# High and low parts of the projected rows in a DRAM region each, 128 rows outermost

## The chip, the cores and the metric

The kernel runs on one core of one Trainium2 chip. The metric is the device time of one execution in microseconds, lower is better. A run of 831.89 us in this document is the median of three executions (829.76 to 833.49).

## What is computed

The reference gates two blocks over the same input `x` (2048 rows of 512): sliding-window attention with 32 heads of 16 columns, and a gated linear unit.

```python
def _A_ref(x, wqkv, wo):
    H = 32; Dh = D // H; W = 256
    q, k, v = ...                       # x @ wqkv, split into heads
    scores = jnp.einsum("bhqd,bhkd->bhqk", q, k) * (Dh ** -0.5)
    mask = (idx[:, None] - idx[None, :] >= 0) & (idx[:, None] - idx[None, :] < W)
    p = _softmax(jnp.where(mask[None, None], scores, -1e9), axis=-1)
    return merge_heads(jnp.einsum("bhqk,bhkd->bhqd", p, v)) @ wo

def _B_ref(x, w_gate, w_up, w_down):
    return (_sigmoid(x @ w_gate) * (x @ w_up)) @ w_down      # F = 1376

g = _sigmoid((x * gate_w).sum(-1, keepdims=True))
return g * _A_ref(...) + (1 - g) * _B_ref(...)
```

## The kernel before

All products are made from split operands: each float32 value is a high part (rounded by ScalarE) and a low part (the rest, by VectorE), and a product is the sum of three matmuls of such parts.

**The work.** Heads come in 8 groups of 4 (`NG`, `HG`), tokens in 16 blocks of 128 (`NB`) and in 4 chunks of 512 (`NC`). A *step* `s` is one group and one chunk, 32 in all. For each step the q and k rows are projected into a PSUM tile `pj`; `proj_hi` (L270) and `proj_lo` (L280) leave the high and low parts in SBUF tiles `sh` and `sl` of 128 partitions by 1024 columns, which hold two neighbouring steps, a *pair*.

**The ring.** The score matmuls read a tile `ring` with 3 slots (`RING`), each for one pair. In a slot, every fourth partition holds a row-wise different thing: rows 1 to 3 of each four hold high and low parts of q and k, row 0 holds the running maximum of a query (with its high and low part), so that one matmul of 64 rows gives the score and subtracts the maximum as well. The parts have to change partitions on the way from `sh` and `sl` to the ring. For the first two pairs DMAs do this directly from SBUF (`stack_build`). From the third pair on (14 pairs) the way leads through DRAM: once both halves of a pair are made, `proj_lo` queues two stores of 512 KB to `stack_scratch`, one for `sh` and one for `sl` (L287), and `stack_load` (L289) queues five loads from it into the ring, 1.5 MB in all, with a small fill from `fill_scratch`.

**The loop.** The main loop (L795) runs over *units* `u`, one per group and block, 128 of them and 10 more. In a unit, `s_part` makes scores of a block of queries against up to three blocks of keys, for their maximum alone (matmul L342, then VectorE's reduction L348). `st_part` makes, 9 units later, the scores again, keys as rows, with the maximum subtracted by the ring's rows (matmul L390, then ScalarE's exponential L395 into `pbuf`). Between these, half-height matmuls of the projections and of the gated linear unit (`gu`, L255) fill TensorE.

**The way of the maxima.** Every four units there is a *visit* (L813): `pv_part` multiplies the probabilities with v (L424), `max_split` makes the negated maxima on VectorE and transposes them into `nt` (L363), and `max_store` (L366) sends `nt` to DRAM. `max_load` (L373) then brings them back into row 0 of the ring in two DMAs. The next block of `st_part` needs them.

**The queue.** Nearly all DMAs are issued by SyncE (SP) in the order written here, by `run_dmas` (L316) over the list `later` and over the loads in `sdma`. SP waits, before each, until its data are ready, and all that is written behind it waits too. In a visit the order is: what is left in `later`, `max_store`, then the output of the attention (`ob` to `oT_scratch` in four DMAs, its sums to `sum_scratch`), then `max_load`, then up to three loads of the stack. The stores of a pair stand in `later` some units ahead of every second visit.

After the 128 units comes a last stage (L965): the gated hidden rows are read back from `gu_scratch` and `tail_scratch`, multiplied with `w_down`, and the attention's output with `wo`.

Of the kernel before, what the change touches and what calls it, by code (L numbers as in the profile page):

```python
# [7 lines left out]
F32 = mybir.dt.float32  # L8
# [6 lines left out]
P = 128  # L15
# [21 lines left out]
RING = 3  # L37
CH2 = 2 * CH
# [3 lines left out]
QB = 32  # L42
# [15 lines left out]
def gated_mix_kernel(  # L58
# [11 lines left out]
    nc = tc.nc  # L70
# [22 lines left out]
    gu_d = nc.dram_tensor("gu_scratch", (2, NFM, P, T), F32, kind="Internal").ap()  # L93
    tail_d = nc.dram_tensor("tail_scratch", (NB, P, 2 * TF), F32, kind="Internal").ap()
    max_d = nc.dram_tensor("max_scratch", (NG * NC, P // QB, HG, 2, 4, QB), F32, kind="Internal").ap()
    stack_d = nc.dram_tensor("stack_scratch", (RING, 4, 2, QB, CH2), F32, kind="Internal").ap()
    fill_d = nc.dram_tensor("fill_scratch", (2, CH2), F32, kind="Internal").ap()

    cpool = ctx.enter_context(tc.tile_pool(name="cpool", bufs=1))
# [37 lines left out]
    with ExitStack() as actx:  # L137
# [44 lines left out]
        def fill_rows(r, which, v):  # L182
            dst = ring[r].bitcast(F32).rearrange("(a r) j f -> r a j f", r=32)[0, :, 2 * which:2 * which + 2]
            return dst, fill_d[v:v + 1].partition_broadcast(8).rearrange("(a j) o f -> a j (o f)", j=2)
# [65 lines left out]
        later = []  # L250
# [29 lines left out]
        def proj_lo(s):  # L280
            sh, sl = parts.pop(s)
            nc.vector.tensor_tensor(sl, pj.pop(s), sh.bitcast(F32), op=ALU.subtract)
            t = s // 2
            made[t] = made.get(t, 0) + 1
            if t > 1 and made[t] == 2:
                for low, v in enumerate(stg.pop(t)):
                    later.append((stack_d[t % RING, :, low], v.bitcast(F32)))  # L287

        def stack_load(t):  # L289
            assert made[t] == 2  # L290
            rows = ring[t % RING].bitcast(F32).rearrange("(a r) j f -> r a j f", r=4)
            dmas = [fill_rows(t % RING, 0, 0)]
            if t < RING:
                dmas.append(fill_rows(t, 1, 1))
            for r, low, js in ((0, 0, (0, 4)), (1, 1, (0, 2)), (1, 0, (2, 4)), (2, 0, (0, 2)), (2, 1, (2, 4))):
                js = slice(*js)
                dmas.append((rows[r + 1, :, js], stack_d[t % RING, js, low].rearrange("j a f -> a j f")))
            return dmas

        def stack_build(t):  # L300
# [141 lines left out]
        def proj(s):  # L442
            for k in range(3 * ND):
                proj_mm(s, k)
            proj_hi(s)
            proj_lo(s)
# [28 lines left out]
        for s in (0, NC):  # L475
            for k in range(3 * ND):
                proj_mm(s, k)
        proj_hi(0)
        proj_lo(0)
        proj_raw(NC)  # L480
        proj(1)
# [87 lines left out]
        def proj_post(s):  # L569
            proj_hi(s)  # L570
            behind.append(lambda: proj_lo(s))
# [223 lines left out]
        for u in range(N):  # L795
# [11 lines left out]
            if u % 8 == 1 and u > 8 and u // 8 + 1 < NP:  # L807
                sdma = stack_load(u // 8 + 1)
# [112 lines left out]
        def blocks(v):  # L921
            return v.rearrange("p (d t) -> p d t", d=ND)

        def free_slot(h, d, c):
            return slot(h, d, c).bitcast(F32)
# [6 lines left out]
        rows = [blocks(free_slot(0, k, 3)) for k in range(2)]  # L932
# [32 lines left out]
        for n, (c, f) in enumerate(steps):  # L965
# [45 lines left out]
            for t in range(4):  # L1011
                r = slice(t * QB, (t + 1) * QB)
# [67 lines left out]
```

## Time and profile before

| what | value |
|---|---|
| median of 3 runs | 831.89 us (829.76 to 833.49) |
| the profiled execution's own time | 831.66 us |
| its span, first to last instruction | 829.9 us |
| TensorE (PE) busy | 757.0 us, 91% of the span |
| VectorE (DVE) busy | 488.0 us, 59% |
| ScalarE (ACT) busy | 425.0 us, 51% |
| GpSimd (POOL) busy | 167.0 us, 20% |
| DMA moved | 118.30 MB, mean 143 GB/s |
| stores to `stack_scratch` | 28 of 512 KB |
| loads from `stack_scratch` into the ring | 14 of 512 KB, 56 of 256 KB |
| mean granted TensorE clock | 0.942 |

The chain that ended last is the work followed back from the last instruction, at each step to what released it. "Idle before" is the time an engine did nothing ahead of an instruction. `PEclk` is the share of TensorE's full clock that was granted. `DMA share` is the mean busy share of the core's 16 DMA engines: 0.25 is four engines' worth. SPq is the time that SP took to issue a DMA.

### The profile page before, as it was taken

What the parts mean: (1) busy time and instruction counts of PE and PEld (TensorE: products, weight loads), DVE (VectorE), ACT (ScalarE), POOL (GpSimd) and SP (SyncE); (2) the same over time, 40 slices, a digit from 0 to 9 for tenths busy, and PEclk for the clock granted to TensorE, in tenths of its full rate; (3) what the DMA queues carried; (4) which work ended last, traced back from release to release, by engine and by line L of the source; (5) the groups of instructions that cost most, each with busy time, mean ns of one, the idle gap of its engine ahead of it and who ended that gap; (6) DMA issues with size and microseconds to landing.
All of it is one profiled execution on the core that took longest, in us unless ns stands there. A gap on an engine that the chain in (4) does not pass through costs nothing.

```text
span 829.9 us, 17381 instructions
## 1 busy us (share of the span) xinstructions
PE 757.0 (91%) x6298; PEld 625.1 (75%) x6298; DVE 488.0 (59%) x1455; ACT 425.0 (51%) x890; POOL 167.0 (20%) x255
## 2 busy tenths in 40 slices
PE   9997889798988879897989879949999999999998
PEld 7785777676867768776877758738787888888886
DVE  5386547364756557364646556635685577858482
ACT  6323555364646447454645555626566655535341
POOL 6001222132213123221323222212233200000000
PEclk9999899898989899898989898979999999999999
DMA  8332343434343444535344334443355798869451
GB/s 282 87 110 77 96 141 125 153 111 138 116 140 85 150 114 137 164 99 170 94 138 126 114 99 157 149 127 111 123 163 169 231 232 227 241 146 269 118 126 51
DMA packets 99166, 118.30 MB, mean 143 GB/s; under 512 B 46190, under 2 KB 58990, under 8 KB 99080
## 3 DMA queue, kind: packets, MB, share of 16 engines
q1 hardware_dynamic: 98936, 117.06, 47.9%
q8 instruction: 49, 0.80, 0.4%
q14 instruction: 37, 0.30, 0.1%
q10 hardware_dynamic: 144, 0.13, 0.0%
HBM read 67.34 MB, written 46.67 MB: 137 GB/s over the span
## 4 chain that ended last, share of the span: by engine, by line
PE 74%; DMA 21%; DVE 3%; issue 1%; ACT 0%; SPq 0%; DVEq 0%; ACTq 0%
PE gu L255 20%; DMA max_scratch<-nt 14%; PE pj L255 8%; PE pv L424 6%; PE s L342 5%; PE st L390 5%; PE tp L559 5%; PE pd L88 4%; PE pd L86 4%; PE pd L87 4%; DMA ring<-max_scratch 4%; PE vh L596 2%; DVE junk L348 2%; PE pa L86 2%; PE pa L87 2%; PE pa L88 2%
## 5 line engine op out<-in xcount | busy, mean ns | idle before, releaser
L348 DVE CUSTOM_DVE_ANT_0 junk<-s,mask 128x384 f32<-128x384 f32 (+2 forms) x512 | 272.2, 532 | 239.0 <-PE s L342 181.2
L395 ACT ACTIVATE pbuf<-st 128x384 f32<-128x384 f32 (+2 forms) x512 | 241.6, 477 | 261.9 <-PE st L390 183.3
L255 PE MATMUL gu<-xh,w 64*128 64x512 f32 x1152 | 299.0, 407 | 0.0
L390 PE MATMUL st<-ring 64*128 64x384 f32 (+2 forms) x536 | 177.5, 347 | 65.4 <-DMA ring<-max_scratch 65.4
L255 PE MATMUL gu<-xl,w 64*128 64x512 f32 x576 | 196.1, 406 | 0.0
L401 POOL TENSOR_SCALAR_AFFINE_SELECT pbuf<-pbuf 128x512 f32<-128x512 f32 x128 | 85.0, 664 | 470.5 <-ACT pbuf L395 429.5
L255 PEld LDWEIGHTS gu<-xh,w 64*128 64x128 f32 x1152 | 169.5, 194 | 9.8
L342 PE MATMUL s<-ring 64*128 64x384 f32 (+2 forms) x536 | 170.2, 336 | 0.5 <-DVE mx L348 0.3
L390 PEld LDWEIGHTS st<-ring 64*128 64x128 f32 x536 | 102.4, 196 | 75.7 <-issue 70.5
L342 PEld LDWEIGHTS s<-ring 64*128 64x128 f32 x536 | 100.2, 194 | 19.4 <-DVE mx L348 5.4
L255 PEld LDWEIGHTS gu<-xl,w 64*128 64x128 f32 x576 | 97.2, 195 | 3.5
L255 PE MATMUL pj<-xh,wqh 64*128 64x512 f32 (+1 forms) x228 | 95.2, 444 | 0.0
L255 PE MATMUL pj<-xl,wqh 64*128 64x512 f32 (+1 forms) x228 | 93.5, 436 | 0.0
L424 PE MATMUL pv<-pbuf,V 128*32 128x384 f32 (+2 forms) x1408 | 84.5, 386 | 0.5 <-POOL pbuf L401 0.5
L255 PE MATMUL pj<-xh,wql 64*128 64x512 f32 (+1 forms) x228 | 80.7, 442 | 0.0
L424 PEld LDWEIGHTS pv<-pbuf,V 128*32 128x32 f32 x1408 | 41.4, 110 | 42.0 <-issue 30.7
L407 POOL TENSOR_SCALAR_AFFINE_SELECT pbuf<-pbuf 128x512 f32<-128x512 f32 x112 | 72.8, 650 | 0.0
L86 PE MATMUL pd<-ring,hb 128*128 128x512 f32 x160 | 62.3, 389 | 0.0
L88 PE MATMUL pd<-ring,hb 128*128 128x512 f32 x160 | 62.3, 389 | 0.0
L87 PE MATMUL pd<-ring,hb 128*128 128x512 f32 x160 | 62.2, 389 | 0.0
L82 ACT CAST hb<-V 128x512 fp32r<-128x512 f32 x40 | 24.9, 622 | 57.3 <-DVE V L760 45.5
L255 PEld LDWEIGHTS pj<-xh,wql 64*128 64x128 f32 (+1 forms) x228 | 48.8, 218 | 2.3
(127 smaller groups left out, 1122.2 us busy)
## 6 DMA issues: line engine op xcount, KB each, us to landing
gu_scratch<-sp SPq DMA_DIRECT2D x72, 256.0 KB
V<-gu_scratch SPq DMA_DIRECT2D x36, 512.0 KB
ring<-stack_scratch SPq DMA_DIRECT2D x56, 256.0 KB
stack_scratch<-sh SPq DMA_DIRECT2D x14, 512.0 KB
stack_scratch<-sl SPq DMA_DIRECT2D x14, 512.0 KB
ring<-stack_scratch SPq DMA_DIRECT2D x14, 512.0 KB
guraw<-in_wgu_dram SPq DMA_DIRECT2D x18, 256.0 KB
oT_scratch<-ob SPq DMA_DIRECT2D x128, 32.0 KB
```

What stands on the lines that cost most here:

```text
L86: mm(ps, lh, rh, start=first, stop=False)
L87: mm(ps, lh, rl, start=False, stop=False)
L88: mm(ps, ll, rh, start=False, stop=last)
L255: return mm(pt, (wl if w == 2 else wh)[r, d], (xl if w == 1 else xh)[r, d, c * CH:(c + 1) * CH], start=k == 0 and not second, stop=k == 3 ...
L342: mm(pt[:, (k - k0) * P:(e - k0) * P], lhsT, blk(g, k, hh, 1, e - k), start=k == k0, stop=e == i + 1, skip_group_check=True,)
L348: nc.vector.tensor_tensor_reduce(junk[:, 0:n], pt[:, 0:n], mask[:, 3 * P - n:], scale=1.0, scalar=NEG, op0=ALU.add, op1=ALU.max, accum_out ...
L390: mm(pt[:, (q - j) * P:(e - j) * P], lhsT, blk(g, q, hh, 0, e - q), start=q == j, stop=e == last, skip_group_check=True,)
L395: exps.append(nc.scalar.activation(p_blk(u, hh, 0, n), pt[:, 0:n * P].rearrange("p (b t) -> p b t", t=P), AF.Exp, scale=SCALE,))
L401: nc.gpsimd.affine_select(pbuf[:, s0], pbuf[:, s0], pattern=[[0, HG], [1, P]], compare_op=ALU.is_ge, fill=0.0, base=0, channel_multiplier=-1,)
L407: nc.gpsimd.affine_select(old, old, pattern=[[0, HG], [-1, P]], compare_op=ALU.is_gt, fill=0.0, base=0, channel_multiplier=1,)
L424: mm(pv[32 * hh:32 * hh + 32, (q - q0) * P:(e - q0) * P], Vf[:, v:v + 32], p_blk(g * NB + j, hh, q - j, e - q), start=j == j0, stop=j == q ...
L559: return mm(tp[b][:, 0:TW], (xl if w == 1 else xh)[r, d, b * P:(b + 1) * P], tw[d][int(w == 2)][r, 0:TW], start=k == 0 and not second, sto ...
```

## The change

The scratch tensor gets another shape. Before, it had for each ring slot 4 groups of 32 rows, and within each group first the high and then the low part. Now each slot has two regions, all 128 rows of the high parts and then all 128 rows of the low parts. The store of `sh` or `sl` was written with the shape 4 by 32 by 1024 on the DRAM side (its groups were 256 KB apart); now it is 128 rows of 1024 on both sides, in one piece of 512 KB. The loads read the same rows in the same shape, from their new places.

```diff
-    stack_d = nc.dram_tensor("stack_scratch", (RING, 4, 2, QB, CH2), F32, kind="Internal").ap()
+    stack_d = nc.dram_tensor("stack_scratch", (RING, 2, P, CH2), F32, kind="Internal").ap()
@@ proj_lo
                 for low, v in enumerate(stg.pop(t)):
-                    later.append((stack_d[t % RING, :, low], v.bitcast(F32)))
+                    later.append((stack_d[t % RING, low], v.bitcast(F32)))
@@ stack_load
                 js = slice(*js)
-                dmas.append((rows[r + 1, :, js], stack_d[t % RING, js, low].rearrange("j a f -> a j f")))
+                dmas.append((rows[r + 1, :, js], stack_d[t % RING, low].rearrange("(j a) f -> a j f", a=QB)[:, js]))
```

The instructions of PE, DVE, ACT and POOL stay what they were and where they were. On SP the 28 stores change their shape and nothing changes its place. This is the first visit with such stores, on SP; the names are tiles, `nt` the transposed maxima, `sh` and `sl` the high and low parts:

```order
 L366 DMA max_scratch<-nt_804 128x32
-L316 DMA stack_scratch<-sh_448 4x32x1024
-L316 DMA stack_scratch<-sl_449 4x32x1024
+L316 DMA stack_scratch<-sh_448 128x1024
+L316 DMA stack_scratch<-sl_449 128x1024
 L316 DMA ring<-fill_scratch 4x2x1024 x2
 L316 DMA ring<-stack_scratch 32x4x1024
```

Nothing moved: the stores' outermost dimension goes from 4 to 128, and the load behind them keeps its shape. The next pair's stores, on SP too, stand behind a `max_load` and ahead of stores of `gu` (`sp`):

```order
 L316 DMA sum_scratch<-ob_1124 4x512
 L373 DMA ring<-max_scratch 4x16x32 x2
-L316 DMA stack_scratch<-sh_1140 4x32x1024
-L316 DMA stack_scratch<-sl_1141 4x32x1024
+L316 DMA stack_scratch<-sh_1140 128x1024
+L316 DMA stack_scratch<-sl_1141 128x1024
 L316 DMA gu_scratch<-sp_1_0_1255 128x512
```

Here too only the shape of the two stores differs, and the DMAs around them are in the order they had.

## The prediction

> **What bounds the kernel now.** I read what TensorE waited for, then the chain of waits around one such wait, then SyncE's queue through two neighbouring visits, and then the DMA share in short windows.
>
> ```profile
> PE st L390 <- DMA ring<-max_scratch: 65.4, 14, 10.4
> ```
>
> TensorE (PE) stood idle for 65.4 us in 14 waits, the longest 10.4, all at the score matmul L390 and all for the load of the maxima into the ring. There are also 14 pairs whose parts go through `stack_scratch`. The chain around one wait (start, duration, what):
>
> ```profile
> 258.41 12.49 DMA max_scratch<-nt
> ```
>
> The store of 16 KB of maxima takes 12.49 us to land. What stands before the store is in SyncE's queue, for a visit without stores of a pair (245.00) and the next one with them (258.41):
>
> ```profile
> 245.00 0.32 SPq L366 DMA_DIRECT2D max_scratch<-nt  x1
> 246.43 1.71 SPq L316 DMA_DIRECT2D oT_scratch<-ob  x4
> 248.18 0.57 SPq L316 DMA_DIRECT2D sum_scratch<-ob  x1
> 248.87 1.17 SPq L373 DMA_DIRECT2D ring<-max_scratch  x2
> ...
> 254.25 0.55 SPq L316 DMA_DIRECT2D stack_scratch<-sh  x1
> 255.45 0.54 SPq L316 DMA_DIRECT2D stack_scratch<-sl  x1
> 258.41 0.33 SPq L366 DMA_DIRECT2D max_scratch<-nt  x1
> 261.81 3.77 SPq L316 DMA_DIRECT2D oT_scratch<-ob  x4
> 265.62 0.51 SPq L316 DMA_DIRECT2D sum_scratch<-ob  x1
> 270.98 1.20 SPq L373 DMA_DIRECT2D ring<-max_scratch  x2
> ```
>
> In the plain visit the load is issued 3.87 us after the store of the maxima, so that store had landed by then. In the visit behind a pair's stores it is 12.57 us, and even the issue of four small DMAs takes 3.77 us instead of 1.71. The DMA share tells why:
>
> ```profile
> 252.50:253.30 0.80, 0.80 (x12) 0.71 (x10) 0.53 (x3) 0.80 (x3) 0.80 (x2) 1.00 0.85 328
> 261.60:262.60 1.00, 1.00 (x12) 0.91 (x10) 0.62 (x3) 0.73 (x3) 0.00 (x0) 1.00 0.26 107
> 277.30:280.70 3.40, 3.40 (x33) 3.09 (x30) 2.15 (x7) 2.00 (x5) 1.23 (x2) 0.99 1.01 378
> ```
>
> The last two columns are that share and the rate. While the pair's stores run (261.6 to 262.6) the share is 0.26 at 107 GB/s: four engines at their limit, twelve idle. Their DRAM side has 4 as outermost dimension. A store of `gu`, 128 rows outermost, ran at 0.85 and 328 GB/s just before (252.5), and the loads into the ring at 378 (277.3). A pair's 1.05 MB take 9.8 us at 107 GB/s, and the maxima, issued behind them in the same queue, land only after them.
>
> **The change, term by term.** SyncE issues as many DMAs as before in the same order; the bytes are the same. The stores have 128 as outermost dimension on both sides, as `gu`'s have. At `gu`'s 328 GB/s a pair takes 3.2 us, at the ring's 378 it takes 2.8; nothing in the rows excludes that 4 KB rows are slower, so 107 GB/s (no change) is the other bound. I take 3.2: it is a store too. At 258 the stores are then out by about 254.25 + 3.2 + 0.6 for the issue, 258.1, before the maxima are issued at 258.41.
>
> *The chain afterwards.* `max_load` is then bound by SyncE, which waits for ScalarE's copy of `ob`. It issues the first output DMA at 261.81, and from there the plain visit needs 2.44 us to the load (246.43 to 248.87); 1.97 us after the load's issue TensorE went on (270.98 to 272.95). That makes 261.81 + 2.44 + 1.97 = 266.2. When does TensorE need it? Its idle times say:
>
> ```profile
> 120.74 0.66 PE L390 MATMUL st<-ring 64*128 64x384 f32 x1 [2.64 <-DMA ring<-max_scratch]
> 272.95 0.66 PE L390 MATMUL st<-ring 64*128 64x384 f32 x1 [5.38 <-DMA ring<-max_scratch]
> 532.67 0.41 PE L390 MATMUL st<-ring 64*128 64x384 f32 x1 [1.21 <-DMA ring<-max_scratch]
> 558.48 0.66 PE L390 MATMUL st<-ring 64*128 64x384 f32 x1 [10.43 <-DMA ring<-max_scratch]
> 85.91 0.65 PE L390 MATMUL st<-ring 64*128 64x384 f32 x1 [8.83 <-DMA ring<-max_scratch]
> ```
>
> TensorE ran out at 272.95 - 5.38 = 267.57, so the wait goes with 1.4 us to spare. The two ends of the list are the odd ones. At 558.48 even the store of the maxima was late, behind issues that took long:
>
> ```profile
> 540.53 0.21 DVE L363 STREAM_TRANSPOSE nt<-nm 128x32 f32<-128x32 f32 x1
> 541.60 0.58 ACT L436 COPY ob<-pv 128x512 f32<-128x512 f32 x1
> 545.21 1.14 SPq L366 DMA_DIRECT2D max_scratch<-nt  x1
> ```
>
> The maxima are ready at 540.74 and `ob` at 542.18. From there the same 2.44 + 1.97 give 546.6, against a need at 558.48 - 10.43 = 548.05: again 1.4 us to spare. The first wait is the only one where SyncE itself has to have the stores landed, for the pair's first ring load:
>
> ```profile
> 67.55 0.57 SPq L316 DMA_DIRECT2D stack_scratch<-sh  x1
> 68.83 3.97 SPq L316 DMA_DIRECT2D ring<-fill_scratch  x2
> 78.85 0.64 SPq L316 DMA_DIRECT2D ring<-stack_scratch  x1
> 79.60 1.12 SPq L373 DMA_DIRECT2D ring<-max_scratch  x2
> ```
>
> With the stores out by 71.4, the load can be issued at 72.8 and `max_load` at 73.55. From there to TensorE it is 1.97 us at best, and 6.31 as it was (79.60 to 85.91), so 75.5 to 79.9 against a need at 77.08. That leaves 0 to 2.8 us; I keep 2 us as what remains over all 14 waits. Idle time removed: 65.4 - 2 = 63.4 us.
>
> *The clock.* After the waits TensorE runs at half clock. The windows from each wait's end to the end of the low clock, 13 of them (after the 1.21 us wait there is none):
>
> ```profile
> 85.91:89.60 3.69, 3.69 (x19) 3.69 (x21) 0.65 (x3) 0.98 (x2) 0.00 (x0) 0.50 0.82 282
> 120.74:123.74 3.00, 3.00 (x15) 3.00 (x17) 0.57 (x2) 1.64 (x4) 0.00 (x0) 0.50 0.83 249
> ...
> 558.48:564.06 5.58, 5.58 (x28) 5.58 (x30) 1.76 (x6) 2.94 (x7) 0.00 (x0) 0.50 0.29 91
> sum 65.90, PE 65.87 PEld 65.90 DVE 18.57 ACT 27.82 POOL 0.00; mean PE 5.07 PEld 5.07 DVE 1.43 ACT 2.14 POOL 0.00
> 532.67:547.00 14.33, 14.33 (x141) 11.42 (x143) 10.60 (x34) 10.22 (x22) 3.68 (x6) 1.00 0.77 243
> ```
>
> They are 65.9 us, all busy. What the half clock costs there is read from the chain, a turn of six `gu` matmuls and two of scores, warm and cold:
>
> ```profile
> 541.08 0.70 PE gu L255 x6
> 541.95 0.70 PE gu L255 x6
> ...
> 559.13 1.28 PE gu L255 x6
> 560.73 1.28 PE gu L255 x6
> ```
>
> A turn takes 0.87 us warm and 1.60 us cold, so 65.9 us of cold work are 35.8 us of warm work: 30.1 us go with the waits. The Trainium skill ("TensorE: Matmul & The Clock Gate", Terms) has the penalty as the low-clock time by (1 - K/N), with 0.50 for K/N 33.0 us here, and would give 735. The turns measured are the price that I use.
>
> *What is late next.* In five warm stretches between the waits, of 27 to 29 us each, TensorE has no gap to speak of, and no other engine is near its limit (their sum, busy time by engine):
>
> ```profile
> sum 139.50, PE 139.36 PEld 112.10 DVE 94.73 ACT 90.77 POOL 41.21; mean PE 27.87 PEld 22.42 DVE 18.95 ACT 18.15 POOL 8.24
> ```
>
> TensorE is busy for 139.36 of 139.5 us, VectorE for 68%. The warm pace is therefore TensorE's own, and it is the pace that I expect throughout. The ring's loads, now right behind an earlier `max_load`, run beside warm work; they are used eight units later and hide there. If that cover were gone, their 1.5 MB at 378 GB/s would cost 4 us per pair.
>
> *The sum.* The profiled execution took 831.66 us (0.23 below the median of the three runs). 831.66 - 63.4 - 30.1 = 738.2: I say **738 us**.
>
> **The rivals.**
>
> *A shorter wait stays.* The 1.4 us to spare is thin: if the maxima land 3 us later than reckoned, because 1 MB now stands on all sixteen engines ahead of them, 1.6 us stay in each of 13 visits, 21 us, or 759. For it: the pairs' last store is issued only 3 us before the maxima at 258. Against it: the `gu` stores at 252.5 hold 0.85 of all engines and delay nobody. Whether the clock falls after so short a wait is open between two rows: after 1.21 us it stayed at 1.00 (532.67), after 2.64 us it was low for 3.00 us more (120.74). At that upper price, 3.00 x 0.456 = 1.4 us per visit, it is 777. The skill's same page (Part 1) lets the clock fall only after an idle window of about 3.4 us, which gives 759 alone; the 2.64 us row speaks against that.
>
> *The low clock is a beat of its own.* Low windows come every 37.5 us between 157 and 503, so they could be a limit on load and not the waits' doing. Then only the idle time goes: 831.66 - 63.4 = 768. Against it: at 532.67 the wait is 1.21 us and the clock stays full for the whole stretch.
>
> *The change doesn't spread the stores.* Then all stays: 832. For it only that the code changes a tensor's shape and nothing about engines; against it the 128-row store of `gu`.
>
> *Slower: sixteen writers slow each other.* If sixteen engines take eight neighbouring rows of 4 KB each, their streams stand 32 KB apart in DRAM, where four stood 256 KB apart. If the DRAM gave them together less than the 107 GB/s of now, every transfer, `gu`'s and the weights' too, would queue behind them for longer than now. At 80 GB/s a pair takes 13.1 us, 3.3 more; in 14 visits 46 us, or 878. It decides from 107 GB/s down, a third of what `gu`'s store reached with 8 KB between rows, which speaks against it. [...]
>
> **How the numbers follow.** All waits gone, 728 to 752: 0.75. A shorter wait, 752 to 785: 0.14. A clock of its own, 768: 0.04. No spread, 832: 0.03. Slower, 878: 0.04. The low end is the 733 of both terms in full (65.4 and 33, the half of 65.9) less 5 for the spread of runs and small waits. The high end, 768, takes in the clock's case and half of the shorter waits, so 0.14 is left out. Faster by over 0.5% (about what a measurement of this kernel can tell from no change) sums to 0.93, within it 0.03, slower 0.04.
>
> **What would show it.** Right: the share while a pair's stores run is near 0.85 or above; from the store of the maxima to `max_load`'s issue it is under 6 us in every visit; TensorE's wait for the ring is under 5 us in all; the clock stays at 1.00 from 90 to 565; the output DMAs issue in 1.7 us per four. Wrong: a share of 0.25 beside the stores, a low clock without a wait, or waits for VectorE or `pbuf` in the place of the ring's.

## The result and the profile after

The changed kernel takes **733.36 us**, the median of 6 runs (732.40 to 735.50); the kernel before takes 830.57 in the 6 runs beside them. The ratio is 0.8832, 95% interval 0.8807 to 0.8856: 97 us less. The forecast was 738.

The wait for the ring is gone. First what TensorE waited for in the changed kernel (us in total, times, longest), then two rows of its page, busy time by engine and granted clock:

```profile
PE tp L559 <- ACT pbuf L395: 2.1, 1, 2.1
PE warm_ps L192 <- DVE warm L187: 1.2, 1, 1.2
...
PE st L390 <- DMA ring<-max_scratch: 0.3, 1, 0.3
```

```profile
PE 722.4 (99%) x6298; PEld 588.8 (80%) x6298; DVE 487.3 (67%) x1455; ACT 422.9 (58%) x890; POOL 166.6 (23%) x255
...
PEclk9999999999999999999999999999999999999999
```

65.4 us in 14 waits became 0.3 in one, the low clock has left the span, and TensorE is busy for 99% of it. SyncE's queue of the changed kernel, in the visit that answers to the one at 258 before:

```profile
217.52 0.32 SPq L316 DMA_DIRECT2D stack_scratch<-sh  x1
218.72 0.32 SPq L316 DMA_DIRECT2D stack_scratch<-sl  x1
221.68 0.32 SPq L366 DMA_DIRECT2D max_scratch<-nt  x1
225.06 1.71 SPq L316 DMA_DIRECT2D oT_scratch<-ob  x4
226.81 0.53 SPq L316 DMA_DIRECT2D sum_scratch<-ob  x1
227.45 1.14 SPq L373 DMA_DIRECT2D ring<-max_scratch  x2
```

From the store of the maxima to the issue of their load it is 5.77 us, where it was 12.57, and the four output DMAs issue in 1.71 us, where they took 3.77. The last two columns of two windows are DMA share and GB/s. The first covers these stores from near their start to their end, the second their middle:

```profile
218.50:221.50 3.00, 3.00 (x44) 2.33 (x44) 2.18 (x14) 2.19 (x5) 1.26 (x3) 1.00 0.83 333
219.00:220.40 1.40, 1.40 (x17) 1.21 (x15) 0.95 (x7) 1.10 (x3) 1.02 (x2) 1.00 1.01 410
```

All sixteen engines are at work. From its first packet to its last the pair takes 3.1 us; the pair ahead of the visit at 258 before took 15.0.

### The profile page after: what moved, and what is told of

Same layout as the page of the kernel before. It is cut to its first block, busy times and chain, and to the rows that moved or that the text cites. A ratio compares the mean times of both kernels' runs of the same rounds, so it can differ in the third digit from the quotient of the medians.

```text
span 731.6 us, 17381 instructions
## 1 busy us (share of the span) xinstructions
PE 722.4 (99%) x6298; PEld 588.8 (80%) x6298; DVE 487.3 (67%) x1455; ACT 422.9 (58%) x890; POOL 166.6 (23%) x255
## 4 chain that ended last, share of the span: by engine, by line
PE 96%; DMA 2%; DVE 1%; issue 1%; SPq 0%; ACT 0%; DVEq 0%; ACTq 0%
PE gu L255 27%; PE pj L255 12%; PE pv L424 11%; PE s L342 7%; PE st L390 5%; PE tp L559 5%; PE pd L86 5%; PE pd L87 5%; PE pd L88 5%; PE vh L596 3%; PE pa L86 2%; PE pa L88 2%; PE pa L87 2%; PE vps L462 2%; DMA wdraw<-in_wd_dram 1%
## 5 line engine op out<-in xcount | busy, mean ns | idle before, releaser
L255 PE MATMUL gu<-xh,w 64*128 64x512 f32 x1152 | 281.2, 393 | 0.0
L255 PE MATMUL gu<-xl,w 64*128 64x512 f32 x576 | 186.0, 391 | 0.0
L390 PE MATMUL st<-ring 64*128 64x384 f32 (+2 forms) x536 | 166.8, 328 | 0.3 <-DMA ring<-max_scratch 0.3
L255 PEld LDWEIGHTS gu<-xh,w 64*128 64x128 f32 x1152 | 155.4, 185 | 12.0
L390 PEld LDWEIGHTS st<-ring 64*128 64x128 f32 x536 | 96.1, 184 | 7.8 <-ACT pbuf L395 1.1
L255 PEld LDWEIGHTS gu<-xl,w 64*128 64x128 f32 x576 | 89.7, 185 | 4.2
L255 PE MATMUL pj<-xl,wqh 64*128 64x512 f32 (+1 forms) x228 | 83.1, 393 | 0.0
L255 PE MATMUL pj<-xh,wqh 64*128 64x512 f32 (+1 forms) x228 | 83.0, 393 | 0.0
L255 PE MATMUL pj<-xh,wql 64*128 64x512 f32 (+1 forms) x228 | 70.5, 393 | 0.0
L255 PEld LDWEIGHTS pj<-xh,wql 64*128 64x128 f32 (+1 forms) x228 | 41.2, 185 | 3.0
```

What stands on the lines that cost most here:

```text
L255: return mm(pt, (wl if w == 2 else wh)[r, d], (xl if w == 1 else xh)[r, d, c * CH:(c + 1) * CH], start=k == 0 and not second, stop=k == 3 ...
L390: mm(pt[:, (q - j) * P:(e - j) * P], lhsT, blk(g, q, hh, 0, e - q), start=q == j, stop=e == last, skip_group_check=True,)
```

## The experiments

**The shape or the place.** The change does two things: it gives the stores another shape, and it puts the high and the low parts elsewhere. The first run, `outer4`, keeps the new places and goes back to four groups, with an unused row between them:

```diff
-    stack_d = nc.dram_tensor("stack_scratch", (RING, 2, P, CH2), ...)
+    stack_d = nc.dram_tensor("stack_scratch", (RING, 2, 4, QB + 1, CH2), ...)
-                    later.append((stack_d[t % RING, low], v.bitcast(F32)))
+                    later.append((stack_d[t % RING, low, :, 0:QB], v.bitcast(F32)))
@@ stack_load: the same rows, read from these places
```

> The changed kernel with its two regions for high and low parts, but with one unused row behind each 32, so that a store keeps 4 groups of 32 rows as its DRAM side. Theory (the outermost dimension sets how many DMA engines a store gets): four engines again, 107 GB/s beside the stores, 65 us of waits for the ring, 826 to 836 us. Rival (the places of the parts in DRAM are what counts, for the writes or for the loads): 733 us or near it.

Measured: 829.97 us, ratio to before 1.0005 (0.9978 to 1.0032), with 66.6 us of waits for the ring. While its stores run the share is a quarter again:

```profile
261.60:262.60 1.00, 1.00 (x12) 0.94 (x10) 0.64 (x3) 0.74 (x3) 0.00 (x0) 1.00 0.24 98
```

The second run, `four_stores`, leaves the old places alone and changes the shape, by issuing each store in four pieces of 32 rows:

```diff
-                    later.append((stack_d[t % RING, :, low], v.bitcast(F32)))
+                    later.extend((stack_d[t % RING, j, low], v.bitcast(F32)[QB * j:QB * j + QB]) for j in range(4))
```

> The kernel before, with its layout untouched, but each store issued as four of 32 rows, so that 32 is outermost. Theory: 16 engines, the waits for the ring gone but for what six more issues on SyncE (0.3 to 0.5 us each) cost ahead of the maxima: 733 to 742 us. Rival of the places in DRAM: 831.

Measured: 735.03 us, ratio 0.8866 (0.8825 to 0.8907), one wait of 1.7 us left. The two answer each other: the new places without the shape bring nothing, the shape without the places brings 94 of the 97 us. Of the places in DRAM no effect can be told from the noise.

**Fewer engines than four.** Two groups of 64 rows (`outer2`), by the edit of `outer4` with the first ring load in two:

```diff
-    stack_d = nc.dram_tensor("stack_scratch", (RING, 2, P, CH2), ...)
+    stack_d = nc.dram_tensor("stack_scratch", (RING, 2, 2, 2 * QB + 1, CH2), ...)
@@ proj_lo, stack_load: the same rows, by two groups of 64
```

> As the one with 4 groups, but 2 groups of 64 rows, and the pair's first ring load split in two. Theory: two engines, about 53 GB/s, a pair takes 19.6 us in place of 9.8, each of the 14 waits grows by about 9.8 us: 831 + 137 = 968 us, 930 to 1010. Rival of the places in DRAM: 733 us. A rival by which only a spread over all sixteen matters (any fewer is the same): 831.

Measured: 930.84 us, ratio 1.1233 (1.1173 to 1.1292), at the low end of the theory's range. What TensorE waited for, and a window of that kernel in which the stores run alone:

```profile
PE st L390 <- DMA ring<-max_scratch: 163.8, 15, 15.9
```

```profile
308.00:312.00 4.00, 0.00 (x0) 0.00 (x0) 0.00 (x0) 0.00 (x0) 0.00 (x0) 0.50 0.13 53
```

A share of 0.13 is two engines, and 53 GB/s is half of the 107 that four gave. The outermost dimension counts the engines, and the rival by which any fewer than sixteen is the same falls. The waits grew by 98 us, not by 137. A window of the kernel before shows where the reckoning was off:

```profile
258.00:262.00 4.00, 4.00 (x56) 2.69 (x50) 1.22 (x6) 1.32 (x4) 1.23 (x2) 1.00 0.26 69
```

The four engines were busy, with a share of 0.26, but moved 69 GB/s here, not 107. From its first packet to its last the pair took 15.0 us, not 9.8, and a pair of `outer2` (the one issued at 289.55) took 21.4. So the step from four engines to two made a pair 1.4 times as long, and not twice.

**Half of it.** `high_wide`: the high parts' store with 128 rows outermost, the low parts' with four groups:

```diff
+                    row = stack_d[t % RING, low]        # (4, QB + 1, CH2)
+                    later.append((
+                        row[:, 0:QB] if low else row.rearrange("j a f -> (j a) f")[0:P], v.bitcast(F32)))
```

> Regions apart; the high parts' store has 128 rows outermost, the low parts' 4 groups of 32. Theory (what counts is whether the maxima land before SyncE is ready to issue the load, 5 to 6 us after their store): the low parts alone need 4.9 us on four engines and are issued 3 us or more before the maxima, so nearly all of the gain comes with the half: 733 to 748 us, the first visit's wait the largest left. Rival (the gain goes with the share of bytes moved to sixteen engines): 782.

Measured: 751.62 us, ratio 0.9075 (0.9027 to 0.9122). That is 4 us above the range of the theory and 30 below the rival's 782: half of the bytes brought 78 of the 97 us. TensorE waited 11.6 us for the ring, 5.1 and 6.1 of them in the first and the last of the 14 visits, and the middle ones had next to nothing. In those two SyncE's own issues took long. The first is here; in it the load of the maxima, issued at 73.67, landed 8.42 us later, where TensorE needed it at 77.10:

```profile
68.66 2.61 SPq L320 DMA_DIRECT2D ring<-fill_scratch  x2
71.36 2.19 SPq L320 DMA_DIRECT2D ring<-stack_scratch  x1
73.67 1.67 SPq L377 DMA_DIRECT2D ring<-max_scratch  x2
...
82.66 0.53 SPq L502 DMA_DIRECT2D guraw<-in_wgu_dram  x1
```

The wait is a threshold and not a share: what lands before SyncE is ready costs nothing.

**Twice the bytes on sixteen engines.** `twice` issues each store a second time:

```diff
                     later.append((stack_d[t % RING, low], v.bitcast(F32)))
+                    later.append((more_d[t % RING, low], v.bitcast(F32)))     # read by nobody
```

> The changed kernel with every one of the 28 stores of 128 rows issued a second time, to a scratch tensor that nobody reads: 2.1 MB per pair on sixteen engines, about 6.4 us at 328 GB/s. Theory (the engines' time ahead of the maxima counts, and 6.4 us on sixteen is still less than 9.8 us on four): no wait of more than 1 to 2 us for the ring, 733 to 745 us. Rival (the spare time of 1.4 us per visit is so thin that 3.2 us more of traffic ahead of the maxima show): about 1.8 us in each of 13 visits and some low clock, 757 to 775.

Measured: 737.00 us, ratio 0.8868 (0.8832 to 0.8904), 4.5 us of waits for the ring in 3 visits. The longest wait, 3.0 us in the last visit, is above the 1 to 2 us of the theory. Twice the bytes cost some 4 us on sixteen engines, while the single bytes on a quarter of the engines cost 97. The double stores of a pair were out 5.4 to 7.1 us after their first packet, and the single stores of the kernel before 12.9 to 15.0 us in the first 13 visits. It is this time ahead of the maxima, and not the bytes, that decides.

**The clock.** `fill` is the kernel before, with work of no use put into the waits of 12 visits:

```diff
+                if hh == 0 and u % 8 == 3 and 19 <= u < 108:
+                    for _ in range(16):
+                        mm(pv, xh[:, 0, 0:P], xh[:, 0, 0:CH], start=True, stop=True)
                 if 0 <= u - LAG < NU:
                     st_part(u - LAG, hh ^ 1 if u < NU else hh)
```

> The kernel before, with 16 matmuls of no use (128x512, 0.227 us apart in the warm rows, 3.6 us) ahead of the waiting score matmul in 12 of the 14 visits with stores; the first and last visit are left as they are. The DMA waits stay. Theory (the half clock is the idle time's doing): the low clock is gone in those 12 visits, 26 us less, and 4 us more where the filling is longer than the wait: 809 us, 800 to 818. Rival (the low clock is a beat of its own): 831 to 840 us, with half clock in the same places.

Measured: 811.28 us, ratio 0.9763 (0.9710 to 0.9817). One of the filled visits, and the stretch from 100 to 530 us of this kernel and of the one before (the granted clock is the third number from the end):

```profile
265.91 0.41 PE L391 MATMUL st<-ring 64*128 64x384 f32 x1 [1.67 <-DMA ring<-max_scratch]
```

```profile
100.00:530.00 430.00, 422.28 (x4095) 342.55 (x4091) 257.34 (x894) 244.05 (x541) 115.33 (x183) 1.00 0.44 136
```

```profile
100.00:530.00 430.00, 384.50 (x3740) 318.93 (x3738) 243.88 (x852) 233.27 (x516) 109.99 (x174) 0.92 0.41 127
```

The maxima came no earlier; a wait of 1.67 us stood where 5.38 had been. The clock is 1.00 over the whole stretch, where the kernel before has 0.92. In `fill` it is low only at the waits of the first and the last visit, which were left as they are. More work made the kernel 20 us faster. The low clock is the idle time's doing and no beat of its own.

**Queue or engines.** Two runs ask why the maxima wait behind the stores. In the first, `act_queue`, ScalarE issues the 28 four-group stores; in the second, `max_on_act`, they stay on SyncE and ScalarE issues the store and the loads of the maxima.

```diff
-                nc.sync.dma_start(dst, src)                  # stores of the pair alone, first run
+                nc.scalar.dma_start(dst, src)
-            nc.sync.dma_start(max_d[s]..., nms.pop(s))       # and the loads at L373, second run
+            nc.scalar.dma_start(max_d[s]..., nms.pop(s))
```

> The kernel before with its layout and shape of 4 groups, the 28 stores issued by ScalarE in place of SyncE. Theory A (the maxima wait because they stand behind the stores in the same queue): the waits for the ring shrink to a few us in all, the four engines stay as busy as they were: 735 to 765 us, with something lost where ScalarE's issues take long. Theory B (the four engines are simply full, whichever queue feeds them): 820 to 840 us.

Measured: 838.54 us, ratio 1.0077 (1.0045 to 1.0110). The time is that of theory B, and TensorE's waits for the ring grew to 75.4 us, but what SyncE waited for is neither theory's:

```profile
SPq L316 <- DMA stack_scratch<-sl: 36.0, 8, 5.9
SPq L373 <- DMA stack_scratch<-sl: 23.6, 5, 5.4
...
SPq L373 <- DMA stack_scratch<-sh: 16.5, 2, 9.2
```

SyncE itself waits for the stores to land before it issues the loads of the maxima (L373), though these use none of the stores' data. The instructions of the visit at 266.07 show why: the second of the two loads is to report its landing on the semaphore on which the store of `sl` had still to report. The maxima had landed at 272.99, `sl` landed at 279.49, and that load was issued at 279.56. So the time of this run can't tell the two apart.

> The kernel before with its four-group stores on SyncE, and the store and the two loads of the maxima issued by ScalarE, so that they stand behind no store of a pair in a queue. Theory A (what delays the maxima is their place behind the stores in one queue): waits for the ring fall from 65 us to under 15; ScalarE loses some 2 to 3 us per visit to the landing of its own store: 745 to 795 us. Theory B (four engines that are full delay whatever passes through them, whichever queue it is in): the waits stay at 50 us or more, 815 to 850 us.

Measured: 827.21 us, ratio 0.9963 (0.9939 to 0.9988), within theory B's range again. No wait for the ring is left on TensorE; it waits for ScalarE instead, 55.8 us in 20 times, because ScalarE now stands idle until its own store has landed. ScalarE's queue in a plain visit and in the next, with stores ahead of it:

```profile
242.63 0.32 ACTq L366 DMA_DIRECT2D max_scratch<-nt  x1
...
244.07 1.11 ACTq L373 DMA_DIRECT2D ring<-max_scratch  x2
```

```profile
256.02 0.32 ACTq L366 DMA_DIRECT2D max_scratch<-nt  x1
...
262.51 1.17 ACTq L373 DMA_DIRECT2D ring<-max_scratch  x2
```

The load follows the store after 1.44 us in the one and 6.49 in the other; in the kernel before it was 12.57. The DMA packets of the traces tell the two theories apart. The store of the maxima is 128 packets of data, and with nothing of a pair ahead the last is through 1.05 us after the issue in most visits. Behind a pair's stores it takes 7.0 to 12.1 us in 13 visits of the kernel before (median 9.9), and 4.7 to 6.2 us in the 14 of `max_on_act` (median 5.4). So full engines delay a transfer of another queue too, by some 4 us, and the place behind the stores in SyncE's queue adds about as much again. Each theory has about half. ScalarE's queue, q10, in the windows 256:258.5 and 258.5:262.5 (packets, MB, share of 16 engines):

```profile
q10 hardware_dynamic: 108, 0.01, 2.9%
q10 hardware_dynamic: 36, 0.00, 0.7%
```

These are the 128 packets of data and 16 that report the landing. Three quarters of them, twelve engines' part, are out early; the last quarter is the part of the four busy engines, and it takes until 262.1. In the kernel before, the last quarter goes out between 267.1 and 270.5, as the pair's own packets come to their end at 270.4.

## Why the prediction was right

The mechanism was right at each step of the sum, and the sum came out 4.6 us high. By the spans, 829.9 and 731.6, the change saved 98.3 us, against 93.5 in the sum.

- **The spread.** 328 GB/s was taken for the stores; they run at 333 over their whole length and at 410 in their middle. The 9.8 us that a pair was said to take before were too few: ahead of the visit at 258 it took 15.0. No term of the sum hangs on that. `outer4`, `outer2` and `four_stores` show that the outermost dimension is the cause.
- **The chain afterwards.** The reckoning gave 5.84 us from the store of the maxima to their load (261.81 + 2.44 - 258.41); it is 5.77. The statement that it is under 6 us in every visit did not hold: it is 6.45 in one with stores ahead (130.11 to 136.56), where the four output DMAs took 3.05 us to issue and not 1.7, and 7.11 in one without (from 467.94). TensorE did not wait for either. In the last of the 14 visits the reckoning had 1.4 us to spare. There the way from the first output DMA to the load took 4.07 us (455.31 to 459.38) and not 2.44, and TensorE waited the 0.3 us that are left.
- **The idle time.** 63.4 us were to go, 65.1 went. The 2 us kept for the first visit were too many: there, `max_load` is issued at 71.23, not at 73.55.
- **The clock.** 30.1 us were to go. The same matmuls, found in both traces, took 66.5 us in the 13 cold stretches and take 36.4 now: 30.2 us. The rule of the Trainium skill ("TensorE: Matmul & The Clock Gate", Terms) gave 33.0; the measured cost is nearer to the turns of the chain, 0.46 of the low-clock time and not one half.
- **What the sum had no term for.** The stretches from the end of each cold one to the next wait are shorter by some 4 us in all, 0.25 to 0.45 at 12 of the 14 waits. What it is stays open; no run tests it. The last stage gave 1.3 back, where the wait for `pbuf` is now 2.1 us and was 1.0.
- **What is late next.** Nothing is. TensorE has 0.3 us of waits for the ring, 0.9 for VectorE's maxima and 2.1 for `pbuf`. The ring's loads, issued earlier, are hidden beside warm work as reckoned.

Of the rivals, the shorter wait did not come: even with twice the bytes it was 4.5 us in all. The beat of its own is refuted by `fill`. That the shape does nothing is refuted by the result. Sixteen writers do not slow each other below what four had: they share 333 to 410 GB/s where four had 69 to 107.

The runs bear out one half-sentence of the prediction's first section only in part: that the maxima land late because they stand behind the stores in one queue. In another queue they were late too, by about half as much.

## What to carry to other kernels

Look at the outermost dimension of every large DMA, here on its DRAM side: a layout that puts a group index of 2 or 4 there gets as many engines, and a share near 0.13 or 0.25 at times when only that DMA runs gives it away. The harm shows elsewhere, in the wait of a small transfer that has to pass the same engines, so follow the chain of waits past the transfer that it names to what was issued before it. A wait of a few microseconds on TensorE costs its own length and then a cold stretch; both belong into the sum.

## What the runs showed of the hardware that was not expected

The clock can fall after quite a short wait: it fell for 3.41 us after 1.71 us in `four_stores`, and after 2.29 and 2.40 us in `max_on_act`, but not after 2.34 us in that same run, nor after 2.05 us in the changed kernel or 2.64 us in `outer4`. Every wait of 2.7 us and more in these ten traces was followed by a low clock. The wait of `four_stores`, and a window from there (granted clock third from the end):

```profile
462.52 0.41 PE L390 MATMUL st<-ring 64*128 64x384 f32 x1 [1.71 <-DMA ring<-max_scratch]
462.50:466.00 3.50, 3.48 (x20) 3.50 (x22) 0.99 (x3) 2.07 (x5) 0.00 (x0) 0.60 0.48 145
```

The Trainium skill ("TensorE: Matmul & The Clock Gate", Part 1) has one idle window of about 3.4 us as the condition. Here a wait of half that length was enough.

Engines that are busy need not be moving data at their rate: the four engines of the kernel before had a share of 0.26 both at 69 GB/s and at 107.

A small DMA lands with the slowest of its engines: behind a pair's stores, three quarters of the store of the maxima were through 2.0 to 4.1 us after the issue in the kernel before, and its last packet after 7.0 to 12.1.
